# The first attention step of a fused RWKV-6 and feed-forward kernel, rebuilt

## The chip, the cores and the metric

The kernel runs on one core of a Trainium2 chip. Such a core has five engines with queues of their own: TensorE (PE; its weight loads are shown apart as PEld), VectorE (DVE), ScalarE (ACT), GpSimd (POOL) and SyncE (SP), which issues most of the transfers. Sixteen DMA engines carry the transfers between HBM and SBUF, the on-chip memory of 128 partitions. [...] The metric is the device time of the whole kernel in microseconds; smaller is better. The median over runs counts.

## What is computed

An RWKV-6 attention over 4 sequences, 8 heads, 768 tokens and head size 48, then a feed-forward with the activation h * erf(softplus(h)) on its 3072 x 384 output. Everything is float32 on the chip; the weights of the feed-forward are given as float64.

```python
def _attn_ref(r, k, v, w, u):
    state = np.zeros((B, H, D, D))
    for t in range(S):
        kt, vt, rt, wt = (k[:, :, t], v[:, :, t], r[:, :, t], w[:, :, t])
        cur = np.einsum('bhd,bhe->bhde', u[None] * kt, vt)
        y[:, :, t] = np.einsum('bhd,bhde->bhe', rt, state + cur)
        state = wt[:, :, :, None] * state + np.einsum('bhd,bhe->bhde', kt, vt)
    return y

def _moe_ref(x, w_in, w_out):          # x: 3072 x 384, d_ff 2048
    h = x @ w_in
    sp = np.maximum(h, 0.0) + np.log1p(np.exp(-np.abs(h)))
    return (h * erf(sp)) @ w_out
```

## The kernel before

**Steps.** A step takes 128 tokens of two sequences (NJ = 2, called batches here), all eight heads of each. There are 6 pairs of chunks in time and 2 pairs of sequences, so 12 steps, `s` = 0 to 11. Steps 0 to 3 (`s < DIRECT`), which the change touches, run through `attend` (L625).

**Attention inside a step.** The recurrence is unrolled in six levels (LOG = 6). The tile `in` holds r and k as [128, 2, 8, 128]: partitions are two groups of 64 head channels (48 used), then r or k, then 8 head pairs (4 per batch), then 128 tokens. The tile `w` holds the decays. `prepare` (L267) makes the products of neighbouring decays on POOL (`tot_sb`, L315), and `rk1`, a copy of r and k in which every other token is multiplied by u: in step 0 DVE does r (L284, L288) and ACT does k (L292, L295), a batch at a time. Then, for each level, `level_products` (L452) multiplies k and r on PE into a PSUM tile of the pool `ps_p` (two tiles, `pp0` and `pp1`, two banks each), `scale` (L263, DVE) multiplies half of r and k by decays in place, and the results are gathered in `own` (L668 at level 1, with the mask `first`; L464 at levels 2 to 5; L471 on ACT at level 6). A level's products read what the scaling of the level before wrote, and a scaling waits until the products have read `in`.

After the levels: `from_own` (L486) multiplies `own` by v into `y`, in two parts (swap 1 and 0); eight transposes (L680) bring k to `kT` (L684, ACT); `state_part` (L538) makes the state's two halves from kT and v; `middle` (L712, DVE) is the state after the first half, `faded` (L713, POOL) its decayed form and L715 the next state; `through_state` (L512) adds r times `middle` to `y`. ACT then copies `y` to `y3` and `xT` (L519 to L522), and six small transfers (L526, three from SP, three from ACT) fill the rest of `xT`, the input of the feed-forward.

**Feed-forward.** `hidden` (L777) multiplies `w_in_sb` by `xT` in eight pieces of six matmuls, one piece for each pair of weight rows, into tiles named `m` of the pool `ps_m` (two tiles). The pieces of step s - 1 stand between the levels of step s. `project` (L809) and later `project_fast` (L885) multiply by `w_out_sb`.

**Weights.** Sixteen pairs (8 of `w_in`, 8 of `w_out`) arrive as float64, read as two 32-bit words, 768 KB each, in `words` (three buffers). `convert` (L185) makes float32 of each: ACT scales the high words into the PSUM tile `pp1` (L212) and the low words into `rest` (L214); DVE shifts (L220) and joins them (L228); POOL adds `rest` (L232). The table `CONVERT` (L1000) puts the stages by hand: letters l (load), s (scale), h (shift), o (join), j for h and o, at places 0 to 7 of each step, and at 8 behind it. The first three pairs are loaded before the steps.

**What sets the order.** The order on each engine is that of the program, written by hand. Before the steps SP issues u, `in` of step 0 in two halves by batch, `w` in two, mask, v, three weight pairs, then `in`, `w` and v of step 1. Of all transfers of a queue at most eight are under way: a ninth waits until the one eight places ahead has landed. So that PE stays busy, 20 matmuls of 128 x 128 run at the start (L1026), `keep_busy` (L638) puts two matmuls of zeros (384 and 192 columns) behind every level of step 0, and `stay_warm` (L646) puts single 512-column ones after it.

Of the kernel before, what the change touches and what calls it, by code (L numbers as in the profile page):

```python
# [11 lines left out]
FP32 = mybir.dt.float32  # L12
# [9 lines left out]
NC = 2  # L22
# [39 lines left out]
def kernel(  # L62
# [80 lines left out]

    def load_w(s, parts=1):
        ws[s] = ins.tile([P, JP, C], FP32, name="w")
        n = JP // parts
        for i in range(parts):
            nc.sync.dma_start(
                out=ws[s][:, i * n : (i + 1) * n], in_=rkw[s][:, 2, i * n : (i + 1) * n]
            )  # L150

    def load_step(s, parts=1):
        t = ins.tile([P, 2, JP, C], FP32, name="in")
        vt = ins.tile([P, NH, D], FP32, name="v")
        n = JP // parts
        for i in range(parts):
            nc.sync.dma_start(
                out=t[:, :, i * n : (i + 1) * n], in_=rkw[s][:, 0:2, i * n : (i + 1) * n]
            )
        if s <= DIRECT:  # L160
            load_w(s, parts)
        if not s:
            nc.sync.dma_start(out=mask_sb[:], in_=masks)
        elif s == 2:
            nc.sync.dma_start(out=block_sb[:], in_=block_mask)
            nc.sync.dma_start(out=u_row[:], in_=u_rows)
        nc.sync.dma_start(out=vt[:], in_=v[s])
        loaded[s] = t, vt

    def near_log(s):  # L170
        return NEAR_LOG - (s == DIRECT)
# [13 lines left out]
    def convert(weights):  # L185

        held = {}

        def load(i):
            if i >= len(weights):
                return
            dst, src = weights[i]
            if src.dtype == FP32:
                nc.sync.dma_start(out=dst, in_=src)
                return
            words = wide.tile([P, 2, DM, 2], I32, name="words", bufs=3)
            nc.sync.dma_start(
                out=words[:].rearrange("p i n two -> p i (n two)"), in_=src.bitcast(I32)  # L200
            )
            held[i] = [words]

        def scale(i):
            if i in held:
                words = held[i][0]
                low, high = words[:, :, :, 0], words[:, :, :, 1]
                base = ps_p.tile([P, 2, NP * C], FP32, name="pp1")[:, :, :DM]
                rest = wide.tile([P, 2, DM], I32, name="rest", bufs=2)


                nc.scalar.mul(out=base, in_=high.bitcast(FP32), mul=2.0**-112)  # L212

                nc.scalar.mul(out=rest[:], in_=low.bitcast(U32), mul=2.0**-29)  # L214
                held[i] += [base.bitcast(I32), rest]

        def shift(i):
            if i in held:
                bits = held[i][1]
                nc.vector.tensor_scalar(  # L220
                    out=bits, in0=bits, scalar1=3, scalar2=None, op0=ALU.logical_shift_left
                )

        def join(i):
            if i in held:
                words, bits, rest = held.pop(i)
                into = weights[i][0].bitcast(I32)
                nc.vector.scalar_tensor_tensor(  # L228
                    out=into, in0=words[:, :, :, 1], scalar=-(1 << 31), in1=bits,
                    op0=ALU.bitwise_and, op1=ALU.bitwise_or,  # L230
                )
                nc.gpsimd.tensor_tensor(out=into, in0=into, in1=rest[:], op=ALU.add)  # L232

        stages = {"l": load, "s": scale, "h": shift, "o": join}
        done = dict.fromkeys(stages, 0)
        for _ in range(3):
            load(done["l"])
            done["l"] += 1
        while True:
            what = yield  # L240
            for stage in {"j": "ho"}.get(what, what):
                stages[stage](done[stage])
                done[stage] += 1
            if weights[0][1].dtype != FP32:
                turns["converting"] = 0 < done["s"] and done["o"] < len(weights)
                turns["next"] = 0

    def rows(e, n=D):
        return slice(e * EP, e * EP + n)
# [6 lines left out]

    def scale(s, level):

        in_t, tots = loaded[s][0], ready[s][1]
        half, nb = 1 << (level - 1), JP * C >> level  # L260
        n = 1 if s > DIRECT and level == LOG else 2
        halves = view(in_t[:, 0:2], half, [[JP * C - half, n], [2 * half, nb], [1, half]])
        nc.vector.tensor_mul(  # L263
            halves, halves, view(tots[level - 1], 0, [[1, n], [2, nb], [0, half]])
        )
# [234 lines left out]
    def through_state(s, xT):  # L500
# [18 lines left out]
        nc.scalar.copy(y3[:].rearrange("p (j t) -> p j t", j=NJ), y[:, 1, :, 1])  # L519
        for j in range(NJ):  # L520
            nc.scalar.copy(xT[:, 0:2, j * C : (j + 1) * C], y[:, 0, j])
        nc.scalar.copy(xT[:, 2, :].rearrange("p (j t) -> p j t", j=NJ), y[:, 1, :, 0])  # L522
        for kk in range(KT):
# [6 lines left out]

    def state_part(s, kT, ps):

        vt = loaded[s][1]
        for n in range(JP):
            for h in range(1 if s >= n_steps - SPC else NC):
                for e in range(NE):
                    t = slice(h * HC, (h + 1) * HC)
                    nc.tensor.matmul(  # L538
                        ps[h][rows(e), n, :D],
                        lhsT=kT[t, e * JP + n, :],  # L540
                        rhs=vt[t, n * NE + e, :],
                        start=True,
                        stop=True,
                    )
# [80 lines left out]
    def attend(s, xT, place, behind):  # L625
# [9 lines left out]
        def keep_busy(*columns):  # L635
            zeros = states[1][0][:].rearrange("p n d -> p (n d)")
            for n in columns if not s else ():
                nc.tensor.matmul(  # L638
                    y[:].rearrange("p e j q t -> p (e j q t)")[:, :n], lhsT=ident[:],
                    rhs=zeros[:, :n], start=True, stop=True, skip_group_check=True,  # L640
                )
# [8 lines left out]
        if s == DIRECT:  # L650
            next(following)
        for level in range(near_log(s) + 1 if s == DIRECT else 1, LOG + 1):
            rk = made[:] if level == 1 else RK
            pp = products([P, NE, JP, HC])
            level_products(pp, rk, level)
            if level == LOG and s == DIRECT:
                spread_blocks(s + 1, pp)
            scale(s, level)
            keep_busy(DM, DM // 2)
            if level == 1 and s == 1:  # L660
# [4 lines left out]
            if level == 1:  # L665
                if not s:
                    nc.vector.tensor_copy(out=first[:], in_=mask_sb[:, 0, :])
                nc.vector.tensor_mul(  # L668
                    own[:], got, first[:, None, :].to_broadcast([P, NH, HC])
                )  # L670
            else:
                take_level(own, pp, level)
# [3 lines left out]

        from_own(s, own, 1)
        ps = products([P, JP, P])
        for n in range(JP):
            nc.tensor.transpose(ps[:, n, :], K[:, n, :], ident[:])  # L680
        if not s:
            stay_warm()
        kT = att.tile([P, NH, D], FP32, name="kT", bufs=1)
# [13 lines left out]

        if s:

            ps = products([P, NC, JP, HC], 1 if s == 1 else None)  # L700
            ps = [ps[:, h] for h in range(NC)]
        else:
            ps = [ps_m.tile([P, JP, HC], FP32, name="m") for h in range(NC)]
        state_part(s, kT, ps)
        from_own(s, own, 0)
        if not s:
            stay_warm(1, products([P, NP * C]))
        for e in range(NE):
            if c:
                nc.vector.tensor_add(middle[rows(e)], faded[0][rows(e)], ps[0][rows(e), :, :D])  # L710
            else:
                nc.vector.tensor_copy(middle[rows(e)], ps[0][rows(e), :, :D])  # L712
        nc.gpsimd.tensor_mul(faded[1][:], middle[:], ends[:, :, 1:2].to_broadcast([P, JP, D]))  # L713
        for e in range(NE):
            nc.vector.tensor_add(S_next[rows(e)], faded[1][rows(e)], ps[1][rows(e), :, :D])  # L715
        for _ in following:
# [255 lines left out]
    def run_late(s, tokens, following=None):  # L972
# [27 lines left out]
    CONVERT = (  # L1000
        ("", "", "", "", "", "s", "jls", "j", "sl"),
        ("hl", "jsl", "jsl", "jsl", "jl", "sj", "", "", "sl"),
# [15 lines left out]
    nc.vector.memset(sums[:], 0.0)  # L1018
    nc.sync.dma_start(out=u_sb[:], in_=u)
    load_step(0, NJ)  # L1020
    with tc.manual_schedule(
        engines={getattr(mybir.EngineType, x) for x in ("PE", "DVE", "Activation", "Pool", "SP")}
    ):
        warm = ps_m.tile([P, P], FP32, name="m")
        for _ in range(20):
            nc.tensor.matmul(warm[:], lhsT=ident[:], rhs=ident[:], start=True, stop=True)  # L1026
        for t in (*states[0], *states[1], middle):
# [12 lines left out]
        next(conversion)  # L1040
        load_step(1)
        for s in range(n_steps):
            xTs[s] = xs.tile([P, KT, UNIT], FP32, name="xT")
# [155 lines left out]
```

## Time and profile before

| What | Value |
|---|---|
| Median of 3 runs | 597.92 us (597.72 to 598.07) |
| Profiled execution | 598.5 us |
| Its span | 596.3 us |
| PE busy | 584.7 us, 7290 matmul records |
| ACT busy | 361.8 us |
| DVE busy | 440.1 us |
| First feed-forward piece (L777) | starts 34.40 us |
| Step 0, level 6 products (L452) | 23.42 to 24.18 us |
| DMA in 11 to 14 us | 416 GB/s |

The profiled execution has a time of its own, a little above the median; the span is its part between the first and the last instruction. Times in traces count from the span's start. A matmul in float32 shows as two records, so the 64 records of a level are 32 matmuls. "issue" in the chain of waits is time in which the engine waited for nothing that the profile shows.

A few rows of the trace that date step 0, with start, duration, engine, line, operation and size:

```profile
5.29 0.43 DVE L284 TENSOR_TENSOR rk<-in,u_sb 128x256 f32<-128x256 f32 x1 [3.04 <-DMA in<-in_rkw]
6.68 1.08 ACT L292 ACTIVATE rk<-in,u_sb 128x64 f32<-128x64 f32 x4 [4.46 <-DMA in<-in_rkw]
...
31.22 0.37 ACT L519 COPY y<-y 128x256 f32<-128x256 f32 x1 [1.17 <-PE y L512]
...
32.17 1.86 SPq L526 DMA_DIRECT2D xT<-y  x3
```

In brackets stands how long the engine was idle before, and what ended that.

### The profile page before, as it was taken

What the parts mean: (1) busy time and instruction counts of PE and PEld (TensorE: products, weight loads), DVE (VectorE), ACT (ScalarE), POOL (GpSimd) and SP (SyncE); (2) the same over time, 40 slices, a digit from 0 to 9 for tenths busy, and PEclk for the clock granted to TensorE, in tenths of its full rate; (3) what the DMA queues carried; (4) which work ended last, traced back from release to release, by engine and by line L of the source; (5) the groups of instructions that cost most, each with busy time, mean ns of one, the idle gap of its engine ahead of it and who ended that gap; (6) DMA issues with size and microseconds to landing.
All of it is one profiled execution on the core that took longest, in us unless ns stands there. A gap on an engine that the chain in (4) does not pass through costs nothing.

```text
span 596.3 us, 16645 instructions
## 1 busy us (share of the span) xinstructions
PE 584.7 (98%) x7290; PEld 501.7 (84%) x7290; DVE 440.1 (74%) x516; ACT 361.8 (61%) x473; POOL 274.5 (46%) x296
## 2 busy tenths in 40 slices
PE   8889999999999999999999999999999999999997
PEld 7667788678758758898898898898898898898997
DVE  5688598799996799799799799799799525023140
ACT  2547788717534398765765666666666664746710
POOL 4348365610588549749449449449459000000000
PEclk9999999999999999999999999999999999999999
DMA  8377381541315324334334335334331300000000
GB/s 320 124 278 234 118 290 58 217 141 20 134 38 159 66 95 168 71 108 169 72 107 168 73 106 169 73 107 134 71 107 54 71 9 26 2 21 13 2 27 26
DMA packets 51376, 63.33 MB, mean 106 GB/s; under 512 B 34920, under 2 KB 40296, under 8 KB 49896
## 3 DMA queue, kind: packets, MB, share of 16 engines
q1 hardware_dynamic: 50824, 62.03, 32.3%
q8 instruction: 57, 0.93, 0.6%
q10 hardware_dynamic: 480, 0.25, 0.2%
q14 instruction: 15, 0.12, 0.1%
HBM read 52.39 MB, written 8.69 MB: 102 GB/s over the span
## 4 chain that ended last, share of the span: by engine, by line
PE 88%; DVE 6%; issue 2%; ACT 2%; DMA 1%; POOL 1%; SPq 0%; DVEq 0%; ACTq 0%; POOLq 0%
PE m L777 40%; PE m L885 28%; PE m L809 8%; PE pp L452 6%; PE y L486 2%; DVE in L263 2%; PE pp L538 1%; PE y L512 1%; DMA in<-in_rkw 1%; PE pp L680 1%; DVE sums L367 1%; DVE words L381 1%; DVE own L464 1%; ACT rk L292 1%; DVE w_in_sb L228 0%
## 5 line engine op out<-in xcount | busy, mean ns | idle before, releaser
L777 PE MATMUL m<-xT,w_in_sb 128*128 128x256 f32 x1152 | 257.3, 382 | 2.3 <-DVE w_in_sb L228 1.3
L777 PEld LDWEIGHTS m<-xT,w_in_sb 128*128 128x128 f32 x1152 | 216.0, 190 | 34.5 <-issue 3.7
L786 ACT COPY h<-m 128x512 f32<-128x512 f32 x96 | 55.6, 580 | 84.2 <-PE m L777 84.1
L263 DVE TENSOR_TENSOR in<-in,tot_sb 128x1024 f32<-128x1024 f32 (+1 forms) x60 | 78.3, 1305 | 24.9 <-PE pp L452 23.8
L377 POOL TENSOR_TENSOR rk<-words 128x528 f32<-128x528 f32 (+3 forms) x28 | 41.6, 1485 | 91.4 <-DVE sums L367 81.0
L381 POOL TENSOR_TENSOR words<-words,rest 128x528 f32<-128x528 f32 (+10 forms) x77 | 79.1, 1027 | 6.0
L809 PE MATMUL m<-w_out_sb,h 128*128 128x384 f32 x192 | 64.3, 491 | 0.0
L809 PEld LDWEIGHTS m<-w_out_sb,h 128*128 128x128 f32 x192 | 35.7, 190 | 23.6
L885 PE MATMUL m<-mixed,h 128*128 128x192 f32 x288 | 51.1, 331 | 0.0
L885 PE MATMUL m<-w_out_sb,h 128*128 128x192 f32 x288 | 50.3, 329 | 0.0
L733 ACT ACT_TABLE_LOAD x36 | 46.2, 1283 | 2.4 <-issue 1.7
L885 PEld LDWEIGHTS m<-w_out_sb,h 128*128 128x128 f32 x288 | 46.9, 190 | 0.5
L885 PEld LDWEIGHTS m<-mixed,h 128*128 128x128 f32 x288 | 46.6, 190 | 0.9
L737 ACT ACT_TABLE_LOAD x36 | 46.2, 1283 | 1.7 <-DVE room L868 1.1
L452 PEld LDWEIGHTS pp<-in 48*64 48x64 f32 (+1 forms) x2368 | 34.0, 125 | 14.8 <-issue 8.1
L885 PE MATMUL m<-w_out_sb,room 128*128 128x192 f32 x256 | 44.2, 326 | 0.0
L452 PE MATMUL pp<-in 48*64 48x64 f32 (+1 forms) x2368 | 38.7, 212 | 4.0 <-issue 1.8
L315 POOL TENSOR_TENSOR tot_sb<-tot_sb 128x256 f32<-128x256 f32 (+4 forms) x60 | 40.4, 674 | 4.5
L885 PEld LDWEIGHTS m<-w_out_sb,room 128*128 128x128 f32 x256 | 42.0, 190 | 0.0
L742 DVE TENSOR_TENSOR h<-h,y 128x1024 f32<-128x1024 f32 x17 | 20.7, 1215 | 28.3 <-ACT y L737 28.2
L733 ACT ACTIVATE room<-h 128x1024 f32<-128x1024 f32 x36 | 38.1, 1057 | 0.4
L742 DVE TENSOR_TENSOR h<-h,pp 128x1024 f32<-128x1024 f32 x19 | 23.1, 1213 | 19.3 <-ACT pp L737 19.2
(123 smaller groups left out, 826.3 us busy)
## 6 DMA issues: line engine op xcount, KB each, us to landing
in<-in_rkw SPq DMA_DIRECT2D x11, 1024.0 KB, 5.1
words<-in_moe_w_in SPq DMA_DIRECT2D x8, 768.0 KB, 5.5
words<-in_moe_w_out SPq DMA_DIRECT2D x8, 768.0 KB, 4.6
words<-in_rk_rows SPq DMA_DIRECT2D x8, 768.0 KB, 6.2
w<-in_rkw SPq DMA_DIRECT2D x11, 512.0 KB, 7.0
v<-in_v SPq DMA_DIRECT2D x12, 384.0 KB, 6.0
out<-o SPq DMA_DIRECT2D x24, 192.0 KB, 2.4
rest<-in_w_rows SPq DMA_DIRECT2D x8, 384.0 KB, 5.0
```

The source lines that it names most:

```text
L263: nc.vector.tensor_mul(halves, halves, view(tots[level - 1], 0, [[1, n], [2, nb], [0, half]]))
L315: nc.gpsimd.tensor_mul(new, pair[:, :, 0], pair[:, :, 1])
L377: engine.tensor_mul(terms[n], r[:, :, n:], k[:, :, : near - n])
L381: engine.tensor_mul(k[:, :, :m], k[:, :, :m], w[:, :, n : n + m])
L452: nc.tensor.matmul(pp[s0 : s0 + m, e, n, :m], lhsT=rk[rows(e), 1, n, s0 : s0 + m], rhs=rk[rows(e), 0, n, t0 : t0 + m], start=True, stop=True,)
L733: nc.scalar.activation(sp_room, chunks[0], AF.Softplus)
L737: nc.scalar.activation(at, sp_room, AF.Erf)
L742: nc.vector.tensor_mul(h, h, at)
L777: nc.tensor.matmul(ps[:, ff, :], lhsT=w_in_sb[:, g * FG + f + ff, kk * P : (kk + 1) * P], rhs=xT[:, kk, :], start=kk == 0, stop=kk == KT - 1,)
L786: nc.scalar.copy(h[:, f : f + FT, :], ps[:])
L809: nc.tensor.matmul(ps[j][:], lhsT=gs[g][:, f, j * C : (j + 1) * C], rhs=w_out_sb[:, g * FG + f, :], start=g + f == 0, stop=g == NG - 1 and ...
L885: nc.tensor.matmul(to, lhsT=a[:, f], rhs=b[:, f], start=start and f == 0, stop=f == FG - 1, skip_group_check=True,)
```

## The change

Line numbers of the new kernel differ; names are the same where a function is kept.

- **Loads of step 0.** `load_first` replaces `load_step(0, NJ)`: `in` of batch 0 first, then u, then r of batch 1, `w` of batch 0, k of batch 1, `w` of batch 1, mask and v.
- **Loads by quarters.** For steps 1 to 3 and for all weight pairs a load is cut along the partitions: `in` and each weight pair into four transfers of 32 partitions, `w` into two of 64. The rows keep their length.
- **Order of loads.** One weight pair instead of three is loaded ahead of step 1's inputs; pairs 1 and 2 follow them, pair 3 comes behind step 0's `xT`.
- **First two weight pairs.** Their high words go to two tiles of `ps_m`, the feed-forward's banks, instead of `pp1`; scaling (ACT), shift and join (DVE) run in halves. The stage "s" splits into "b" (high) and "r" (low). Pair 0 is scaled at place 0 of step 0 and the low words of pair 1 at place 1; pair 0 is joined at place 5, pair 1's high words are scaled just before `through_state` and joined at place 7.
- **Scalings in parts.** In step 0 level 1 is scaled a batch at a time, level 6 k first and then r.
- **After the levels of step 0.** The transposes come ahead of y's first part, behind which a fence (a small DVE copy of `y`) is put. Only half of the state is made ahead of `through_state`, and the other half and the next state after it. `middle` is copied by ACT and DVE, a half each; of the xT copies ACT keeps one and DVE gets two. `first` is made by ACT.
- **Filler matmuls.** 3 matmuls of 512 columns instead of 20 of 128 at the start; one of 512 columns instead of two (384 and 192) behind levels 1 to 5, none behind level 6; two `stay_warm` matmuls of step 0 go.

```diff
-    def load_step(s, parts=1):
+    def load_rows_of(dst, src, parts):
+        n = P // parts
+        for i in range(parts):
+            nc.sync.dma_start(out=dst[i * n : (i + 1) * n], in_=src[i * n : (i + 1) * n])
+    def load_w(s):
+        ws[s] = ins.tile([P, JP, C], FP32, name="w")
+        load_rows_of(ws[s], rkw[s][:, 2], 2 if s < DIRECT else 1)
+    def load_first():
...
+        nc.sync.dma_start(out=t[:, :, b0], in_=rkw[0][:, 0:2, b0])
+        nc.sync.dma_start(out=u_sb[:], in_=u)
+        nc.sync.dma_start(out=t[:, 0, b1], in_=rkw[0][:, 0, b1])
+        nc.sync.dma_start(out=ws[0][:, b0], in_=rkw[0][:, 2, b0])
+        nc.sync.dma_start(out=t[:, 1, b1], in_=rkw[0][:, 1, b1])
+        nc.sync.dma_start(out=ws[0][:, b1], in_=rkw[0][:, 2, b1])
+        nc.sync.dma_start(out=mask_sb[:], in_=masks)
+        nc.sync.dma_start(out=vt[:], in_=v[0])
+    def load_step(s):
...
+        load_rows_of(t, rkw[s][:, 0:2], 4 if s < DIRECT else 1)
...
-            nc.sync.dma_start(
-                out=words[:].rearrange("p i n two -> p i (n two)"), in_=src.bitcast(I32)
+            load_rows_of(
+                words[:].rearrange("p i n two -> p i (n two)"), src.bitcast(I32), 4
             )
...
-        def scale(i):
+        def scale_high(i):
             if i in held:
+                high = held[i][0][:, :, :, 1].bitcast(FP32)
+                if i < 2:
+                    base = [ps_m.tile([P, NP * C], FP32, name="m")[:, :DM] for _ in range(2)]
+                    parts = [(base[n], high[:, n], n) for n in range(2)]
+                else:
+                    base = ps_p.tile([P, 2, NP * C], FP32, name="pp1")[:, :, :DM]
+                    parts = [(base, high, slice(0, 2))]
+                for to, of, _ in parts:
+                    nc.scalar.mul(out=to, in_=of, mul=2.0**-112)
...
-        for _ in range(3):
-            load(done["l"])
-            done["l"] += 1
+        load(0)
+        done["l"] += 1
...
-    def scale(s, level):
+    def scale(s, level, batch=None, only=None):
+        if batch is not None:
+            nb //= NJ
+            halves = view(
+                in_t[:, 0:2], half + batch * NP * C,
+                [[JP * C - half, 2], [2 * half, nb], [1, half]],
+            )
...
+        if only is not None:
+            halves = view(in_t[:, only], (1 - only) * half, [[2 * half, nb], [1, half]])
...
+        if not s:
+            nc.scalar.copy(by_kk[0], y[:, 0, :, 0])
+            nc.vector.tensor_copy(out=by_kk[1], in_=y[:, 0, :, 1])
+            nc.vector.tensor_copy(out=by_kk[2], in_=y[:, 1, :, 0])
...
-            keep_busy(DM, DM // 2)
+            if level < LOG:
+                keep_busy(2 * C)
...
-        from_own(s, own, 1)
+        if s:
+            from_own(s, own, 1)
         ps = products([P, JP, P])
         for n in range(JP):
             nc.tensor.transpose(ps[:, n, :], K[:, n, :], ident[:])
         if not s:
-            stay_warm()
+            from_own(s, own, 1)
+            fence()
...
+        state_part(s, kT, ps, (0,) if not s else range(NC))
         from_own(s, own, 0)
         if not s:
-            stay_warm(1, products([P, NP * C]))
+            nc.scalar.copy(middle[rows(1)], ps[0][rows(1), :, :D])
+            nc.vector.tensor_copy(middle[rows(0)], ps[0][rows(0), :, :D])
+            fade()
+            conversion.send("b")
+            through_state(s, xT)
+            place(LOG + 1)
+            state_part(s, kT, ps, (1,))
+            to_next()
+            for _ in following:
+                pass
+            behind()
+            return
...
     CONVERT = (
-        ("", "", "", "", "", "s", "jls", "j", "sl"),
+        ("s", "r", "", "", "", "j", "", "jl", "sl"),
...
-        for _ in range(20):
-            nc.tensor.matmul(warm[:], lhsT=ident[:], rhs=ident[:], start=True, stop=True)
+        for _ in range(3):
+            nc.tensor.matmul(
+                warm[:], lhsT=ident[:], rhs=ident[:, None, :].to_broadcast([P, NP, P]),
+                start=True, stop=True,
+            )
...
         load_step(1)
+        for _ in range(2):
+            conversion.send("l")
```

Here `fade` is the old POOL instruction for `faded[1]` and `to_next` the two old DVE additions for the next state, as functions.

## The prediction, made before the changed kernel ran

> **What bounds the kernel now.** I read the page's engine shares first, then busy time by windows, then the chain of waits over the first 70 us, then SyncE's queue.
>
> ```profile
> span 596.3 us, 16645 instructions
> PE 584.7 (98%) x7290; PEld 501.7 (84%) x7290; DVE 440.1 (74%) x516; ACT 361.8 (61%) x473; POOL 274.5 (46%) x296
> ...
> PE   8889999999999999999999999999999999999997
> ```
>
> TensorE (PE) bounds the kernel: of 596.3 us it lacks only 11.6. The three 8s in the strip say where: the first 45 us.
>
> ```profile
> 11.00:14.00 3.00, 2.75 (x82) 1.90 (x85) 2.86 (x4) 0.00 (x0) 1.27 (x5) 1.00 1.01 416
> 32.00:35.00 3.00, 1.74 (x12) 0.61 (x5) 2.94 (x4) 1.06 (x3) 0.57 (x1) 1.00 0.13 35
> 200.00:300.00 100.00, 100.00 (x1182) 83.21 (x1181) 90.03 (x109) 72.73 (x91) 64.04 (x75) 1.00 0.34 104
> ```
>
> Columns: stretch, length, busy PE, weight load, VectorE (DVE), ScalarE (ACT), GpSimd (POOL), granted clock, DMA share, GB/s. From 200 to 300 PE is never idle, so a stream that begins earlier ends earlier by as much. The first row gives the rate of full-height loads, 416 GB/s; the second shows clock 1.00 with PE 42% idle.
>
> ```profile
> 6.68 0.59 ACT rk L292 x2
> ...
> 9.06 0.33 ACT rk L295
> ...
> 9.42 1.23 DVE in L263
> 10.65 0.53 DVE first L667
> ...
> 14.73 0.72 issue
> ...
> 20.75 0.62 issue
> ...
> 28.43 1.83 POOL w_in_sb L232
> ...
> 33.33 0.96 DVE w_in_sb L228
> ...
> 34.40 1.28 PE m L777 x4
> 35.71 1.97 PE m L777 x8
> ```
>
> Step 0 is this chain (start, length, what): ACT's multiplications by u, six rounds of scaling and products with two PE stalls, then weight conversion mixed with the state, until the first feed-forward piece runs from 34.40 to 37.68. What the change can win is what it takes off this chain.
>
> ```profile
> 6.58 0.33 SPq L157 DMA_DIRECT2D in<-in_rkw  x1
> 7.72 0.33 SPq L148 DMA_DIRECT2D w<-in_rkw  x1
> 8.39 0.33 SPq L167 DMA_DIRECT2D v<-in_v  x1
> ```
>
> These three issues wait for the transfer eight places ahead of each (SyncE waits 0.8, 0.8 and 0.3 us for `in`, `w`, `w`). So they date landings: second half of `in` 6.56, of `w` 7.70 and 8.37.
>
> **The change, part by part.**
>
> *First loads.* u no longer goes first (its issue took 0.39), so `in` starts 0.45 earlier and its first half lands at 5.29 - 0.45 = 4.85. Batch 1 now comes as r, w of batch 0, k: five quarter megabytes instead of four before k is complete, 6.56 + 0.64 - 0.45 = 6.75 at the 1.27 us per half megabyte between 5.29 and 6.56, or 7.25 if the 1.14 us of the first `w` piece is typical; I take 7.1. ACT waited until 6.68 for both halves though it reads one; the split by r and k lets it begin batch 0 at 5.0. Its block of five lasts 1.39 (6.68 to 8.07), so k of batch 1 ends at 7.1 + 1.39 = 8.5 instead of 9.39.
>
> *Warm-up and level 1.* 3x512 columns replace 20x128: 1536 for 2560, 60% of 7.1 us, ending near 6; no one waits. First products' second half: 8.5 + 0.56. The first scaling comes in two halves of about 0.65; batch 0 runs beside ACT, batch 1 ends near 9.2 (before 10.65). `first` (0.53 on the chain) moves to ACT, idle until the mask lands. The filler matmul is 512 columns instead of 576, 1.17 x 512/576 = 1.04 us, and now sets level 2: 8.5 + 0.56 + 1.04 = 10.1, before 11.23. Gain 1.1.
>
> *Levels 2 to 6.* Unchanged: 2.57 a level (18.67 less 16.10), and about 0.95 more where PE stalls ("issue" 0.72 and 0.62). Instruction packets move 2 to 6 us ahead of such stalls, and later while DMA is full: PE's next instructions come late. Counting products, stalls are 128 matmul records apart, so one falls in level 4; the next, in level 6, comes when loads have ended. Level 6's products end at T = 10.1 + 4x2.57 + 0.75 + 0.95 = 22.1; without a stall 21.1, with two 23.0. Before: 24.2, so 2.1 are gained; I go on with 22.1.
>
> *From T to the first feed-forward piece.* k is scaled first (0.65), so eight transposes run from T+0.7 to T+1.7, ACT's copies of `own` (1.18) beside them; y's first products 0.6 to T+2.4. ACT copies kT (0.81) to T+2.6; half of the state, 32 matmuls, to T+3.1. DVE meanwhile: second scaling 0.65, shift and join of pair 0 in halves (0.97 + 0.95, some 0.03 more each time it is cut) to T+3.4, the fence 0.1. ACT's half of `middle` (0.57) ends at T+3.7, DVE's behind it at T+4.3; through the state 0.6 to T+4.95; y3 and the first xT copy on ACT to T+5.7; two xT copies on DVE, behind ACT's read of the same bank, to T+6.45. Three xT issues per queue at 0.62 to 0.72, 2.2 us to landing: first at T+8.0, last T+9.1. DVE then shifts and joins pair 1 to T+8.45. The stay-warm matmul, 1.05 us, reuses that pair's bank, so it waits for the join's first half at T+7.95 and ends at T+9.05; behind it on PE stands the feed-forward. The piece then runs at 2.79 without waits for xT (before 3.27) to T+11.9 = 34.0. Before 37.68: gain 3.7, of which 1.6 in this part.
>
> *What is moved.* DVE gets the fence and two xT copies (0.75 together) and loses `first` (0.60). Scaling pair 0 (1.8 us) and the low half of pair 1 (0.92) run on ACT while it waited for level 6 (idle 9.4 us up to 18.82); without this cover they would return to the chain, as at 25.43 before. In SyncE's queue pairs 1 and 2 move behind step 1's inputs, and pair 3 behind xT: issued at T+7.7 = 29.8 instead of 28.36, wanted near 37. A quarter load is four issues of 0.33 for one, 1.0 us more per pair, while a pair is wanted every 3.9. Later steps keep their order. In step 1 DVE starts its scaling at T+9.6 after the state's two additions (1.12); scaling, masking, shift, scaling, join and take (1.23 + 1.22 + 0.96 + 1.23 + 0.95 + 1.34 = 6.93, and 0.1 for PE) put level 3's products at 38.7, before 42.33: 3.6 of the gain are left.
>
> *Loads by quarters.* No row of this trace has a large transfer on 32 or 64 partitions. Bounds: 416 GB/s, and 230, the worst quarter megabyte here (262,144 bytes in 1.14 us; the next took 0.67, 391 GB/s). I take 391 or more: the quarters keep rows of 6 and 8 KB, the slow piece had 2 KB, and up to eight follow each other in one queue. Above 294 GB/s it costs nothing (rival A).
>
> [...] The trace does not decide; its full-height loads alone are shown.
>
> *Sum.* The profiled execution is 598.5 (span 596.3 and 2.2 around it); less 3.6 gives 594.9. It lies 0.6 above the median of 597.92, so the median becomes 594.3.
>
> **Rivals.**
>
> *A. The quarters are slow, and the first step waits for weights.* ACT's low scaling of pair 1 stands ahead of its copies of `own`. First loads land at 9.25 (`w` at 8.37 - 0.45, then 0.56 MB of mask and `v` at 416); then, until pair 1 has landed, `v` (0.95) and 3.15 MB in parts: pair 0 0.79, `in` 1.05, `w` 0.52, pair 1 0.79. At 230 GB/s that is 9.25 + 13.7 + 0.95 = 23.9, the scaling ends at 24.8, the `own` copies at 26.0 and the y products 2.3 later than T+1.7 = 23.8. Then 3.93 MB until pair 5 (pairs 3, 4, `in`, `w`) take 17.1 + 0.95 from 29.8 + 2.3 = 32.1 to 50.2, wanted at 47.69 - 3.6 + 2.3 = 46.4: 3.8. In step 2 the like 3.15 MB and `v` go from 68.95 (pair 10's issue) to pair 11 at 83.6, used at 81.89: 1.7. Sum 3.6 - 2.3 - 3.8 - 1.7 = -4.2: 602.1. It decides below 294 GB/s (3.93 MB in 44.1 - 29.8 - 0.95 = 13.35 us) and makes the kernel slower below about 255. For it: all loads of steps 1 to 3 change. Against it: one slow piece of two.
>
> *B. Only part arrives.* Step 1's DVE work per level, 1.23 + 0.96 + 0.95 + 0.73 = 3.87, is as long as PE's 2.79 + 1.09, so there is no slack for a late pair; or the quarters run between 260 and 294. At 270 A's terms lose 0.2 and 1.2; with a second PE stall (1.0) the gain is 1.2: 596.7. Against: pair 5 had landing 5.5 after issue at 40.99 and was used at 47.69, slack 1.2.
>
> *C. The clock falls* with fewer warm-up columns and ACT's wait at level 1. If six levels of products (1.1) doubled, 6.6 less 3.6 is 3.0 slower: 600.9. Against: the granted clock is 1.00 in the 32 to 35 row.
>
> *D. The change doesn't do what it says,* the joins staying on DVE's path: then the tail's 1.6 are gone, 595.9. Against: each half has a bank of its own and ACT is free early.
>
> **How the numbers follow.** Forecast 0.60, A 0.22, B 0.10, D 0.05, C 0.03. The forecast's own range is a stall more or less (1.0) and 0.4 for the first loads: 592.9 to 595.7. A by the quarters' rate runs from 598 to 603. Eight in ten: 592.8 to 600.2, which takes B and the milder half of A. A measurement of this kernel can tell 0.2%, 1.2 us, from no change: faster (under 596.7) 0.68, within 0.10, slower (over 599.1) 0.22.
>
> **What would show it.** Right: ACT's first multiplication near 5.0, level 2's products near 10, one "issue" stall by level 4, level 6 done near 22, ACT's low scaling of pair 1 before that, first feed-forward piece ending near 34, PE gapless after 70. Wrong: GB/s between 10 and 18 us near half of 416, ACT's `own` copies behind a DMA wait, or ACT's scalings in step 1 released by `words` transfers. A gain far over 4 would mean that the old loads delayed something I have not priced, such as the instruction packets beyond level 6.

## The result and the profile after

The change made the kernel slower: median 618.85 us (618.22 to 621.99, 6 runs) against 597.99 us for the kernel before on the same chip (597.65 to 598.11, 6 runs), a ratio of 1.0356 [1.0335, 1.0378]. The forecast was 594.3 us; the sign is rival A's, but A ended at 602.1. The profiled execution has a span of 617.2 us, 20.9 more than before. Of all runs below one alone, 688.27 us of e6_interleaved at a granted clock of 0.84, was in a slower state of the chip; it is left out of that kernel's median.

From the page of the changed kernel: span, busy times, and the strips of PE and of its granted clock (40 slices of 15.4 us).

```profile
span 617.2 us, 16644 instructions
PE 589.3 (95%) x7238; PEld 499.8 (81%) x7238; DVE 443.7 (72%) x523; ACT 361.5 (59%) x475; POOL 270.4 (44%) x296
...
PE   7877986999999999999999999999999999999997
...
PEclk7798997999999999999999999999999999999999
```

PE has 52 matmul records fewer and yet 4.6 us more busy time (589.3 for 584.7): it ran slower. The other 16.3 of the 20.9 are idle time, and 15.6 of it lies before 120 us (23.4 us without PE there, 7.8 before the change), in the first seven or eight slices, where the strip has no row of 9s yet.

Windows of the changed kernel, columns as in the prediction (the last three: granted clock, DMA share, GB/s):

```profile
10.00:14.00 4.00, 4.00 (x81) 2.38 (x76) 1.75 (x2) 0.24 (x1) 2.09 (x5) 0.50 1.03 226
14.00:18.00 4.00, 4.00 (x78) 2.38 (x77) 2.47 (x2) 1.80 (x3) 0.00 (x0) 0.50 0.98 227
42.00:60.00 18.00, 13.79 (x252) 11.00 (x247) 10.57 (x11) 4.60 (x7) 7.91 (x5) 0.91 1.04 230
80.00:100.00 20.00, 16.26 (x304) 12.93 (x304) 12.91 (x12) 9.77 (x11) 8.90 (x5) 1.00 0.92 209
120.00:600.00 480.00, 479.03 (x5320) 414.61 (x5311) 364.95 (x434) 296.15 (x362) 218.81 (x242) 1.00 0.28 87
```

Two things stand here. Where the kernel before moved 416 GB/s (11 to 14 us), this one moves 226 to 230, and the share of busy DMA engines is the same 1.0 (0.98 to 1.04 for 1.01): the engines don't show as idle, and carry little more than half as much. And between 10 and 18 us PE is "busy" throughout, at a granted clock of 0.50. From 120 us on next to nothing is lost: PE is busy for 479.03 of 480 us.

The chain of waits over the first 130 us of the changed kernel, its transfers and what stands beside them:

```profile
5.31 8.36 DMA words<-in_moe_w_in
...
13.68 8.12 DMA w<-in_rkw
...
33.89 4.04 DMA xT<-y
...
38.82 4.61 DMA words<-in_moe_w_in
...
43.49 8.61 DMA w<-in_rkw
...
52.11 7.58 DMA words<-in_moe_w_in
...
84.16 6.47 DMA in<-in_rkw
...
90.65 9.79 DMA words<-in_moe_w_out
```

Before, this chain began with a load of `in` until 6.6 us and then ran through ACT, DVE, PE and POOL up to 45 us; now it jumps from transfer to transfer. Who waits for them is in the timeline of the same kernel (in brackets the wait and what ended it):

```profile
15.44 0.96 ACT L226 ACTIVATE m<-words 128x384 f32<-128x384 f32 x2 [5.10 <-DMA words<-in_moe_w_in]
21.94 1.04 POOL L354 TENSOR_TENSOR tot_sb<-w 128x512 f32<-128x512 f32 x1 [9.48 <-DMA w<-in_rkw]
27.04 0.90 ACT L232 ACTIVATE rest<-words 128x768 int32<-128x768 uint32 x1 [3.54 <-DMA words<-in_moe_w_in]
27.84 1.16 ACT L510 COPY own<-pp 32x512 f32<-32x512 f32 x2
59.80 0.90 ACT L226 ACTIVATE pp<-words 128x768 f32<-128x768 f32 x1 [9.35 <-DMA words<-in_moe_w_in]
100.62 0.84 ACT L226 ACTIVATE pp<-words 128x768 f32<-128x768 f32 x1 [8.41 <-DMA words<-in_moe_w_out]
```

The third and fourth line are the sign that the prediction named for rival A: ACT's copies of `own` behind a DMA wait. The second is one that no case had priced: POOL is idle for 9.48 us until the decays `w` of step 1 land. A number in brackets is idle time and not delay: in the kernel before POOL waited 7.45 us for the same `w` and began at 20.03, so the delay here is 1.9 us.

### The profile page after: what moved, and what is told of

Its sections match the earlier page's. It is cut to its first block, busy times and chain, and to the rows that moved or that the text cites. A ratio compares the mean times of both kernels' runs of the same rounds, so it can differ in the third digit from the quotient of the medians.

```text
span 617.2 us, 16644 instructions
## 1 busy us (share of the span) xinstructions
PE 589.3 (95%) x7238; PEld 499.8 (81%) x7238; DVE 443.7 (72%) x523; ACT 361.5 (59%) x475; POOL 270.4 (44%) x296
## 4 chain that ended last, share of the span: by engine, by line
PE 77%; DMA 11%; ACT 5%; DVE 4%; issue 1%; POOL 1%; SPq 1%; ACTq 0%; DVEq 0%; POOLq 0%
PE m L851 36%; PE m L959 27%; PE m L883 4%; DMA words<-in_moe_w_in 3%; PE pp L491 3%; DMA w<-in_rkw 3%; PE y L525 2%; DMA in<-in_rkw 2%; DMA words<-in_moe_w_out 2%; PE y L551 1%; PE pp L585 1%; DMA xT<-y 1%; PE pp L737 1%; DVE in L302 1%; ACT room L807 1%
## 5 line engine op out<-in xcount | busy, mean ns | idle before, releaser
L851 PE MATMUL m<-xT,w_in_sb 128*128 128x256 f32 x1152 | 261.3, 386 | 9.7 <-ACT h L860 5.6
L851 PEld LDWEIGHTS m<-xT,w_in_sb 128*128 128x128 f32 x1152 | 218.5, 192 | 43.3 <-issue 6.2
L491 PEld LDWEIGHTS pp<-in 48*64 48x64 f32 (+1 forms) x2368 | 36.3, 133 | 22.7 <-issue 10.7
L491 PE MATMUL pp<-in 48*64 48x64 f32 (+1 forms) x2368 | 41.0, 220 | 6.9 <-issue 3.9
L354 POOL TENSOR_TENSOR tot_sb<-tot_sb 128x256 f32<-128x256 f32 (+4 forms) x60 | 39.0, 650 | 4.5
```

The lines of the kernel that those rows point to most:

```text
L354: nc.gpsimd.tensor_mul(new, pair[:, :, 0], pair[:, :, 1])
L491: nc.tensor.matmul(pp[s0 : s0 + m, e, n, :m], lhsT=rk[rows(e), 1, n, s0 : s0 + m], rhs=rk[rows(e), 0, n, t0 : t0 + m], start=True, stop=True,)
L851: nc.tensor.matmul(ps[:, ff, :], lhsT=w_in_sb[:, g * FG + f + ff, kk * P : (kk + 1) * P], rhs=xT[:, kk, :], start=kk == 0, stop=kk == KT - 1,)
```

## The experiments

Theory P: transfers over part of the partitions are slow. Theory K: the clock is what is lost. Others are named where they come in. Ratios are to the kernel before, run on the same chip with the kernels beside it.

**1. All loads over 128 partitions again, the rest of the change kept (e1_full).**

```diff
     def load_rows_of(dst, src, parts):
+        parts = 1
```

> The changed kernel with every load cut along the partitions put back to one transfer over 128 partitions; the order of the loads and all else stay. Theory P (a transfer over 32 or 64 partitions moves at about 230 GB/s instead of 415, and weights and inputs come late): the rate from 10 to 17 us is back near 415 GB/s, the waits for `words`, `w` and `in` in steps 0 to 2 go, 595 to 600 us; the granted clock still falls to 0.5 near 8 us, since PE's idle time there has another cause, and costs some 4 of these. Theory O (the new order of loads, one weight pair ahead of step 1's inputs): 612 us or more. Theory K (the clock of 0.5 from 8 to 22 us is the loss): 612 or more.

599.86 us, ratio 1.0048 [1.0016, 1.0079]. Its window:

```profile
8.00:14.00 6.00, 4.59 (x99) 2.90 (x100) 2.21 (x3) 3.28 (x9) 3.12 (x6) 0.72 1.02 421
```

421 GB/s and 19 of the 20.9 us are back. The clock is still low (0.72), and the kernel is not faster than the one before: with whole loads the forecast gain does not come either.

**2. And the kernel before with nothing but the cuts (e3_before_quarters).** `in` and `w` of step 1 and later and all weight pairs go through `load_rows_of` as in the change; all else is as before.

> The kernel before, with only its loads of steps 1 to 3 and of the weight pairs cut along the partitions as in the change (quarters, w in halves); order, scalings and fillers are the old ones. P: 225 to 240 GB/s from 10 to 25 us, 612 to 622 us with a granted clock of 1.00 in step 0. O or K: 598 us.

617.85 us, 1.0328 [1.0304, 1.0351].

```profile
10.00:14.00 4.00, 3.75 (x95) 2.56 (x87) 3.89 (x5) 0.00 (x0) 2.01 (x4) 1.00 1.03 232
14.00:18.00 4.00, 1.63 (x65) 1.43 (x66) 1.24 (x2) 0.00 (x0) 0.00 (x0) 1.00 1.03 238
```

The cuts alone make 19.4 us of loss (617.85 against 598.46 on this chip), nearly the whole, with the old order of loads and the clock at 1.00 here.

**3. The long start of warm matmuls put back (e4_quarters_warm on the change, e2_full_warm on e1_full).**

```diff
-        for _ in range(3):
-            nc.tensor.matmul(warm[:], lhsT=ident[:], rhs=ident[:, None, :].to_broadcast([P, NP, P]), ...)
+        for _ in range(20):
+            nc.tensor.matmul(warm[:, 0], lhsT=ident[:], rhs=ident[:], start=True, stop=True)
```

> The changed kernel with the 20 matmuls of 128 columns at the start, loads by quarters kept. P: the clock is 1.00 in step 0, but level 6's copies on ACT still wait for the second weight pair near 27 us, so the gain is under 1.5 us: 617 to 619 us. K: under 612.

622.16 us, 1.0384 [1.034, 1.0428], some 3 above what was expected. The clock is 1.00 from 8 to 14 us, and falls when PE next starves:

```profile
14.00:18.00 4.00, 0.84 (x49) 0.76 (x49) 1.05 (x1) 1.74 (x3) 0.00 (x0) 0.94 1.00 225
18.00:22.00 4.00, 3.23 (x38) 1.61 (x40) 1.84 (x2) 1.50 (x5) 0.00 (x0) 0.50 1.07 223
22.00:30.00 8.00, 8.00 (x161) 4.75 (x160) 4.17 (x4) 3.02 (x7) 3.67 (x6) 0.50 0.78 175
```

PE is busy for 0.84 of 4.00 us, and then the clock is 0.50. So in this run the low clock comes behind a wait, and K falls: with the clock at 1.00 up to 22 us e3_before_quarters lost nearly as much as the change, and the long start won nothing here.

> As e1_full, and the 20 matmuls of 128 columns at the start instead of 3 of 512; the filler behind the levels stays at one of 512. P with the clock as a second, smaller term: granted clock 1.00 throughout, level 2's products near 11.1 us, level 6 done near 23, 594.5 to 596.5 us, 3 to 5 below e1_full. If the clock costs nothing: as e1_full.

597.63 us, 0.9994 [0.9977, 1.001], clock 1.00, and 1.1 above the expected range. With whole loads the short start had cost 2.2 us (599.86 less 597.63). But now nothing is left of the gain of 3.6 either. Its chain of waits, and two rows of its timeline:

```profile
14.72 0.83 issue
...
20.98 0.48 issue
...
23.40 0.78 PE pp L492 x50
...
34.27 1.93 DVE in L303
...
33.77 2.92 PE L852 MATMUL m<-xT,w_in_sb 128*128 128x256 f32 x12
...
33.30 1.82 POOL L256 TENSOR_TENSOR w_in_sb<-w_in_sb,rest 128x768 int32<-128x768 int32 x1 [3.14 <-DVE w_in_sb L252]
```

The same scaling and addition in the kernel before:

```profile
34.20 1.22 DVE L263 TENSOR_TENSOR in<-in,w 128x1024 f32<-128x1024 f32 x1
...
34.43 2.67 POOL L232 TENSOR_TENSOR w_in_sb<-w_in_sb,rest 128x768 int32<-128x768 int32 x1 [3.28 <-DVE w_in_sb L228]
```

Both PE stalls are still there, level 6 ends at 24.2 as before, and where the tail is 1.0 shorter (the piece ends at 36.7) VectorE's scaling of step 1 starts at 34.27 (before 34.20) and takes 1.93 instead of 1.22, beside a GpSimd addition that began 1 us earlier. In the kernel before the order was the reverse: the scaling began first and the addition took 2.67 instead of 1.82.

**4. As many transfers as in the change, but cut along the row, 128 partitions each (e5_free_split).** `load_rows_of` cuts columns: `dst[:, i * n : (i + 1) * n]`.

> The changed kernel with the same number of transfers of the same size for steps 1 to 3 and the weight pairs, but cut along the row: each covers all 128 partitions, with rows a quarter (w: half) as long. Theory P (partitions): about 415 GB/s from 10 to 17 us, 598 to 602 us, like e1_full; pieces of 1.5 to 2 KB may cost some per cent of the rate. Rival N (four times as many transfers, each waiting for the one eight places ahead, and more issue time): 225 to 260 GB/s and 612 us or more.

601.98 us, 1.0053 [1.0028, 1.0078].

```profile
10.00:14.00 4.00, 4.00 (x82) 2.38 (x74) 1.38 (x2) 2.46 (x5) 1.77 (x5) 0.50 1.06 388
```

With as many transfers of the same size the rate is 388 GB/s where the quarters had 226, so the halved rate does not come from their number or size.

**5. The same quarters issued in the order 0, 2, 1, 3 (e6_interleaved).**

> The changed kernel with its quarters issued in the order 0, 2, 1, 3, so that a quarter of the lower 64 partitions and one of the upper 64 follow each other. [...] If the sixteen engines work through the queue in step, or a transfer over few partitions is slow in itself, nothing changes: 225 to 240 GB/s, 616 to 622 us.

613.89 us, 1.025 [1.0216, 1.0284]: 2 us below the case in which nothing changes.

```profile
10.00:14.00 4.00, 3.65 (x96) 2.00 (x100) 3.10 (x4) 0.57 (x2) 1.85 (x5) 1.00 1.03 280
14.00:18.00 4.00, 2.87 (x109) 1.90 (x103) 2.60 (x3) 2.01 (x5) 0.00 (x0) 1.00 1.01 259
```

Alternating between the halves helps a little, 259 to 280 GB/s or 14 to 24% over the 226 and 227 of the change, and far from doubles the rate.

**6. Weight pairs whole, inputs still cut (e8_words_whole).** In `load` the 4 becomes 1.

> The changed kernel with the weight pairs whole again (one transfer over 128 partitions each), in and w of steps 1 to 3 still cut. By bytes, 12.6 MB of weights are quick again and 4.7 MB stay at 230 GB/s, which costs 9 us of transfer more than whole loads in three portions of 3: P gives 602 to 608 us. If the share of the loss did not follow the bytes but lay in the inputs (they stand ahead of the weights in the queue): 612 or more.

612.02 us, 1.0208 [1.0178, 1.0238]: 4 us above P's range and at the edge of the other case. Of the loss 13.4 us stay with the inputs alone (612.02 against 598.58 on this chip). Two rows of its chain of waits:

```profile
18.34 2.77 issue
...
89.08 7.55 DMA words<-in_moe_w_out
```

Whole weight pairs that stand in the queue behind cut inputs are still waited for (7.55 us), PE stalls for 2.77 us in step 0, and the clock is 0.50 from 22 to 26 us. How the 13.4 us divide among these was not tried.

**7. Halves of 64 neighbours instead of quarters of 32 (e10_halves64).**

> The changed kernel with inputs and weight pairs cut into two transfers of 64 partitions instead of four of 32. Theory P (the rate goes with the partitions that a transfer covers): GB/s between 10 and 18 us lies between the 225 to 240 of the quarters and the 388 to 421 of full height, some 260 to 350, and the time between 602 and 615. Rival N (any cut along the partitions costs the same, as it is the place where a transfer starts and not how many partitions it covers): 225 to 250 GB/s and 616 to 622. Rival H (only 32 partitions are slow, 64 are as good as 128): 380 to 421 GB/s and 599 to 602.

622.47 us, 1.0406 [1.0365, 1.0446].

```profile
10.00:14.00 4.00, 4.00 (x80) 2.38 (x76) 1.50 (x2) 0.00 (x0) 1.90 (x5) 0.50 1.01 226
14.00:18.00 4.00, 4.00 (x84) 2.06 (x80) 3.06 (x3) 1.80 (x3) 0.00 (x0) 0.77 1.01 221
```

Against what P said as I had put it: 64 partitions are as slow as 32 (226 and 221 GB/s for 226 and 227), so from 32 to 64 neighbours the rate does not grow. Whether any transfer under 128 is slow (rival M below) is still open here.

**8. The same numbers of partitions, spread over all 128 (e11_strided).**

```diff
-            nc.sync.dma_start(out=dst[i * n : (i + 1) * n], in_=src[i * n : (i + 1) * n])
+            nc.sync.dma_start(out=dst[i::parts], in_=src[i::parts])
```

> The changed kernel with the same number of partitions in each transfer as before (32 for a quarter of inputs and weights, 64 for a half of w), but not neighbours: quarter i takes partitions i, i+4, i+8 and so on, half i takes i and every second one, so that each transfer reaches from partition 0 to 127. Theory S (what is slow is that all rows of a transfer lie in one half of the partitions, so that transfers of 32 and of 64 neighbours are equally slow, as the halves of 64 showed with 221 to 232 GB/s): 370 to 421 GB/s between 10 and 18 us, and 599 to 602.5. Rival M (a transfer is slow because it covers fewer than 128 partitions, wherever they are): 220 to 250 GB/s and 615 to 622. [...]

601.68 us, 1.0052 [1.0036, 1.0069].

```profile
10.00:14.00 4.00, 4.00 (x79) 2.36 (x68) 1.50 (x2) 1.79 (x3) 1.99 (x5) 0.57 0.95 345
14.00:18.00 4.00, 3.29 (x76) 1.57 (x79) 3.92 (x4) 3.49 (x10) 1.29 (x1) 1.00 0.97 358
```

M falls: 32 partitions in a transfer, but taken every fourth, run at 345 to 358 GB/s (a little under the 370 expected), and 17 us are back. Slow, at 221 to 241 GB/s, were transfers of neighbouring partitions that all lie in one half of the 128. Two things stay open: no run tried neighbours on both sides of the middle (32 to 95, say), and this edit takes every fourth row from HBM as well, so the runs do not tell the place in SBUF from the place in HBM.

**9. Those loads with the long start (e12_strided_warm).**

> e11_strided, and the 20 short warm matmuls of the kernel before instead of three wide ones: the change with both suspected defects taken away and its parts by quarters kept. If S holds and parts by quarters are worth nothing in themselves: as e2_full_warm, 597.3 to 598.5, PE's clock 1.00 throughout. If earlier landing of parts helps the weight conversion or the inputs of step 1: below 597. If four issues for one cost something on SyncE's queue: 599 to 602, with the first feed-forward piece later than 33.8. Under rival M: 615 to 622.

602.31 us, 1.0074 [1.0059, 1.009], no faster than e11_strided, and near the case of the four issues, though its sign was not seen: the first piece starts at 32.21, not later than 33.8. The first step does end early, level 6 at 22.6 us and step 1's level 3 at 40.66 (before 42.33), and PE starves later (12.30 of 15 us busy between 45 and 60, against 14.86 in e2_full_warm). SyncE's issues in its timeline:

```profile
31.34 5.04 SPq L148 DMA_DIRECT2D words<-in_moe_w_in  x8
36.48 2.97 SPq L148 DMA_DIRECT2D in<-in_rkw  x4
39.55 1.18 SPq L148 DMA_DIRECT2D w<-in_rkw  x2
```

At 0.6 us an issue, step 2's `w` is issued at 39.55; in e2_full_warm at 34.85.

**10. Parts only for step 1's loads and weight pairs 0 to 2, whole loads after that, `w` likewise, on e12_strided_warm (e13_parts_first).**

```diff
-        load_rows_of(t, rkw[s][:, 0:2], 4 if s < DIRECT else 1)
+        load_rows_of(t, rkw[s][:, 0:2], 4 if s < 2 else 1)
...
+                4 if i < 3 else 1
```

> e12_strided_warm with parts (every fourth or second partition) only for the loads of step 1 and of weight pairs 0 to 2; all later loads are whole. Theory Q (the loss of e12_strided_warm against the kernel before comes from the many issues on SyncE's queue from 31 us on, and the first step's gain of 1.7 us at step 1's level 3 is real): PE loses nothing between 45 and 100 us that the kernel before doesn't lose, level 3's products of step 1 start near 40.7, and the time is 596.0 to 597.0. Rival R (the first step is only early because later work was left behind, in the weights or on DVE, and gives it back within step 1): level 3 near 40.7 too, but 597.5 to 599. Rival F (the early end of the first step was chance, a packet of instructions that came early once): level 6 ends near 24 and 597.5 to 598.5.

596.65 us (596.04 to 599.7, 12 runs) against 598.33, ratio 0.9976 [0.9965, 0.9986]: faster than both kernels, though by only 0.24% of the one before. From its windows, and PE in its timeline:

```profile
10.00:14.00 4.00, 3.65 (x116) 2.05 (x115) 3.09 (x3) 1.84 (x3) 1.49 (x5) 1.00 0.99 375
42.00:60.00 18.00, 17.85 (x292) 14.76 (x291) 14.32 (x16) 14.56 (x26) 15.18 (x11) 1.00 0.68 231
...
21.79 0.76 PE L492 MATMUL pp<-in 48*32 48x32 f32 x64 [0.35 <-DVE in L303]
35.90 1.16 PE L492 MATMUL pp<-in 48*64 48x64 f32 x64 [0.67 <-DVE own L725]
40.62 1.16 PE L492 MATMUL pp<-in 48*64 48x64 f32 x64 [0.77 <-DVE own L504]
```

Step 1's level 3 starts 1.7 us before the kernel before's 42.33, PE lacks 0.15 us between 42 and 60 (0.80 in the kernel before, 2.70 in e12_strided_warm), and the span is 1.7 shorter (594.6 for 596.3). Theory Q holds; R and F fall.

**11. GpSimd's addition of pairs 0 and 1 in two halves (e9_add_halves on e2_full_warm, e14_parts_first_add on e13_parts_first).**

```diff
-                nc.gpsimd.tensor_tensor(out=into, in0=into, in1=rest[:], op=ALU.add)
+                for n in range(2) if i < 2 else [slice(0, 2)]:
+                    nc.gpsimd.tensor_tensor(out=into[:, n], in0=into[:, n], in1=rest[:, n], op=ALU.add)
```

> e2_full_warm (full-height loads, 20 short warm matmuls) with one edit: GpSimd adds the low words of pairs 0 and 1 in two halves instead of one, so that VectorE's scaling of step 1 does not stand beside one long addition. Theory V (in e2_full_warm the tail's gain went into VectorE's scaling, 1.93 us instead of 1.22, because GpSimd's addition of 1.82 was under way before it): the first half starts as soon as VectorE has joined that half, the scaling runs beside at most a short rest of the second and takes 1.25 to 1.5; step 1's level 2 products start 0.4 to 0.7 earlier than 37.52, and the time is 0.4 to 0.7 below e2_full_warm, 597.0 to 597.3. Rival W (VectorE is slow there for another reason, or two short additions hold it up as one long does): the scaling still takes 1.8 to 1.95 and the time stays at 597.6 to 598.

> e13_parts_first with GpSimd's addition of pairs 0 and 1 in two halves, as in e9_add_halves, where step 1's scaling took 1.59 instead of 1.93 and level 2's products started 0.36 earlier. By theory V: level 3 of step 1 at 40.3, and 0.3 to 0.4 below e13_parts_first, 595.7 to 596.7. If it is hidden anyway: the same as e13_parts_first within 0.2.

The scaling takes 1.59 in e9_add_halves and 1.60 in e14_parts_first_add, and step 1's level 2 starts at 37.16 instead of 37.52 in the first: the long addition that was under way had held it up, by 0.34 of the 1.93. (V had 1.25 to 1.5, W 1.8 and more; it came out between.) In time it can't be seen: 597.99 us, 0.9994 [0.9976, 1.0011], and 596.72 us, 0.9972 [0.9961, 0.9982]. The 9 runs of e14_parts_first_add spread from 595.13 to 598.11, and in its profiled run the first loads came later than in e13_parts_first (level 6's products begin at 22.42 instead of 21.79), so 0.3 either way would be hidden; this stays open.

**12. u from ACT's queue, and k of batch 1 ahead of r, on e2_full_warm (e7_k_first; 17 warm matmuls).**

> As e2_full_warm (all loads over 128 partitions), with u loaded from ACT's queue instead of second in SyncE's, k of batch 1 ahead of r of batch 1, and 17 matmuls instead of 20 at the start. Theory: in e2_full_warm the first step gained nothing by level 6 because k of batch 1 landed at 8.02 us; here it lands near 6.2, the second half of the first products ends near 8.9, level 2 starts near 10 instead of 11.2, and 0.7 to 1.2 us are gained against e2_full_warm: 596.3 to 597.0 us, if DVE's work at the start of step 1 lets it through. If DVE there sets the time whatever step 0 does: 597.6.

598.81 us, 0.9999 [0.9978, 1.0021], above both cases and no gain. Level 2 starts at 10.15, 1.0 earlier than in e2_full_warm, and then:

```profile
13.69 1.21 issue
...
16.64 1.99 PE pp L492 x64
```

PE stalls for 1.21 instead of 0.83 and resumes at 14.9, where it resumed at 15.5 in e2_full_warm; then the clock falls to 0.84 and 0.74 (14 to 18, 18 to 22 us) and a level's products take 1.99 instead of 1.16. Of 1.0 us 0.5 are left at the end of level 6, and none at step 1.

## Why the prediction was wrong

**Loads by quarters.** This step failed, and most of the loss is its doing: "I take 391 or more: the quarters keep rows of 6 and 8 KB". Measured were 226 to 241 GB/s for quarters, 232 to 238 in the kernel before with cuts alone. I argued from the length of a row, of which one slow and one fast quarter megabyte of full height said little, and passed over the only thing that was new, the place of the partitions. With the lower of the two bounds the sign would have been right. But "Above 294 GB/s it costs nothing" was wrong as well: with parts of full height at 378 to 388 GB/s e5_free_split took 601.98, and with whole loads e1_full 599.86. So at the forecast rate the change would still not have been faster; the terms below stood in its way.

**Rival A** was the right mechanism at the right rate, and its prices were too small: 2.3, 3.8 and 1.7 us of delay, 602.1 in all. ACT was idle for 3.54 (pair 1), 9.35 (pair 5) and 8.41 us (pair 11) at these places. The delay against the kernel before says more: ACT's copies of `own` began 3.6 us later (27.84 for 24.22), pair 5 was scaled 12.1 later (59.80 for 47.69) and pair 11 18.7 later (100.62 for 81.89). A's own sums, the gain of 3.6 taken off, had 0.6, 2.5 and 4.2. A also left out `w` of step 1, and that inputs alone are most of it (e8_words_whole: 612.02). It took each delay as if the queue then stood where it did before; in fact xT's issues and the next loads share that queue, so that a late step loads the following one late, and PE was granted a clock of 0.50 from about 8.6 to 22.3 us (over the whole span 4.6 us more of busy time).

**Warm-up and level 1.** "Ending near 6; no one waits" was wrong: the matmuls did end near 6 (6.26), but PE then idled 0.35 and 2.17 us before the products, and its clock was 0.50 from about 8.6 to 22.3 us. With whole loads this was 2.2 us (e1_full against e2_full_warm); with the quarters the long start won nothing (e4_quarters_warm), and between e11_strided and e12_strided_warm, where SyncE's queue came to bind, it made no difference. Rival C named the cause at 0.03 and put 6.6 us on it; the row it was dismissed by (32 to 35 us, clock 1.00 at 58% busy) didn't hold for the start. *First loads:* ACT's first multiplication came at 5.18, as said (5.0); k of batch 1 landed at 8.0, not 7.1, and between 7.5 and 8.4 in kernels with these same loads. So level 2 started at 11.18 in e2_full_warm, where 10.1 was forecast.

**Levels 2 to 6.** One stall of 0.95 was expected; with whole loads there were two, 0.83 and 0.48, in levels 3 and 5, as before (0.72 and 0.62). In e13_parts_first there was one, 0.44, and T was 22.55, near the forecast 22.1. That looser loads let PE's instructions through sooner fits (the second packet of instructions moved between 16 and 17 us there, between 19 and 20 in e2_full_warm and in the kernel before), but was not tested by itself.

**From T to the first piece, and what is moved.** In e13_parts_first the piece ends near T + 12.7 (35.2), 0.8 later than the forecast T + 11.9. VectorE starts step 1's scaling at T + 10.1 (32.66) for T + 9.6, and from there to level 3's products 7.03 became 7.96: the scaling beside GpSimd's addition took 0.70 more, and DVE waited 0.41 for PE where 0.1 was allowed. I priced that scaling at 1.23 from rows where it began first. So the rebuilt step, with its loads and its start mended, is worth 1.7 us of the 3.6: 0.45 of the rest was lost by T, 0.5 behind it and 0.9 from the scaling on. D is half borne out: VectorE's two passes over pair 1 (1.02 and 1.01 us) stand on the chain ahead of that scaling, and from T to the scaling 10.1 us pass, as before (10.0). The whole gain was made by T (24.18 less 22.55), none in the tail. B (260 to 294 GB/s) was passed by, though e6_interleaved ran at its rates (259 to 280) and lost 2.5%, where B left a gain of 1.2 us: the same undershot prices as in A.

**Four issues for one** were put at "1.0 us more per pair, while a pair is wanted every 3.9". In e12_strided_warm an issue took 0.59 us, not 0.33, four of them 2.5 to 3.0 instead of 0.4 to 0.6, the chain of waits runs through these issues from 31.3 to 40.1 us, and whole loads from step 2 on won 5.7 us (602.31 to 596.65). Part of the 5.7 may be the rate, 345 to 364 GB/s for parts and 416 to 422 for whole loads; the two were not separated.

## What to carry to other kernels

When a load is cut into parts, cut it along the row or take every n-th partition, so that each part still spans all 128: here such parts moved 378 to 388 and 345 to 375 GB/s. Parts of 32 or 64 neighbours moved 221 to 241 where whole loads had 416 to 422, and a DMA share of 1.0 hid it, so read GB/s beside the share. Cut only the loads that someone waits for: each part is an issue in its queue (0.59 us in e12_strided_warm), and the next step's loads stand behind it. When a step gets earlier, price the engine that the gain lands on with what then runs beside it (a scaling of 1.22 us became 1.93), and look at the granted clock behind every new wait of TensorE (0.50 behind the change's 2.17 us).

## What the runs showed that was not expected

- A DMA share of 0.98 to 1.06 goes with 221 as with 421 GB/s. Halves of 64 neighbours (221 to 226) were no faster than quarters of 32 (226 to 227), and alternating quarters of both halves reached 259 to 280.
- The granted clock came back late in one kernel and soon in another: in the changed kernel it was 0.50 in each window between 10 and 22 us although PE was busy 4.00 of 4.00 in all three. In e11_strided it was back at 1.00 by 14 us. What decides that was not tried.
- VectorE and GpSimd held each other up at the start of step 1: the same scaling took 1.22 in the kernel before and 1.93 in e2_full_warm, the same addition 2.67 and 1.82, and in both the one that began second paid.
